# A searched instruction order, and remainder slots taken into the row-paired projections, in a fused attention and feed-forward kernel

## The chip, the cores and the metric

The kernel runs on one core of a Trainium2 chip. The metric is the time of the slowest core in microseconds (us), here that of the only one.

## The reference

An attention with random features (8 batches, 8 heads, 576 positions, 64 dimensions, 128 features) is followed by a gated feed-forward block on its 4608 output rows.

```python
def phi(x):                                   # x: q or k, scaled by D ** -0.25
    h = einsum('bhsd,md->bhsm', x, omega) - sum(x * x, -1, keepdims=True) / 2
    return exp(h - max(h, -1)) / sqrt(m)
q_p, k_p = phi(q_s), phi(k_s)
kv  = einsum('bhsm,bhsd->bhmd', k_p, v)
z   = sum(k_p, axis=2)
num = einsum('bhsm,bhmd->bhsd', q_p, kv)
den = einsum('bhsm,bhm->bhs', q_p, z)[..., None] + 1e-6
x   = (num / den).transpose(0, 2, 1, 3).reshape(4608, 512)

h   = x @ w_in                                # 512 -> 2048, the up-projection
g   = h * sigmoid(beta * h)
out = g @ w_out                               # 2048 -> 512, the down-projection
```

All inputs and the output are float32; the kernel computes its matmuls in bf16.

## The kernel before

The kernel is built in two steps. A first pass lists operations with their engine, an estimated duration and the tiles that they read and write. A greedy scheduler then simulates all engines, gives out the eight banks of PSUM (the memory that TensorE writes its results to) and fixes each engine's order. A table of small corrections to the priorities, found by a search, tunes that order.

```python
UPS = 2                                      # up and down blocks alternate in groups of this many
EARLY = 'q0 v0 q1 k1 w0 qm w2 w1 w3 o2 v1 o0 o1 o3'   # early loads: w = w_in, o = w_out, by chunk
HINTS = {1: 3, 3: -3, 8: -1, ...}            # (cut) priority corrections by number of the operation
...
        for op in self.ops:                  # in the scheduler
            op.prio += HINTS.get(op.seq, 0)
...
                places = {n: place(n) for n in (1, 2, 4)} if e == "PE" else None
```

`w_in` and `w_out` come in four chunks of 512 columns or rows each. They stand with the other early loads in the queue of GpSimd, in the order of `EARLY` as the scheduler then places them.

```python
    def load_w_out(c):
        dma("POOL", 0.8, 2.55,
            lambda e: e.dma_start(
                w_out_bf[:, 4 * c : 4 * c + 4, :],
                moe_w_out[c * 512 : (c + 1) * 512, :].rearrange("(f p) d -> p f d", p=128)),
            writes=[("wout", c)])
```

From batch 1 on, q and k are projected in two parts for each half of the positions. An "island" holds the main part: two matmuls of 64 rows each run beside each other, one on the upper and one on the lower half of the array's rows. Four banks take the results. The remainder slot (positions 512 to 575) is projected apart, as a matmul on the whole array with the block-diagonal `bd`, into a bank of its own.

```python
        def island(x, half):
            banks = [Use("att") for _ in range(4)]
            ...
                    for c in range(8):                       # k; q has 4 matmuls of 512 columns
                        for a in range(2):
                            rows = slice(64 * a, 64 * a + 64)
                            i = e.matmul(ps[:, banks[2 * a + c // 4].b, c % 4 * 128 : c % 4 * 128 + 128],
                                         src[rows, c // 4, c % 4, :], bd[rows, a, :], ...)
            ...                                              # then four exponentials on ScalarE
        def proj(x, half, i):                                # i = 4: the remainder
            ...                    # k: 1 matmul of 256 columns; q: 2 of 128; one exponential of 256
...
                    if b >= ISLAND:
                        island(x, half)
                        proj(x, half, 4)
```

The softmax here doesn't subtract the row's maximum and nothing guards it: scores larger than these inputs give would overflow.

## Time and profile before

| | |
|---|---|
| time before, median of the first 3 runs | 321.13 us (320.84 to 321.63) |
| span in the trace (first to last instruction) | 320.3 us |
| TensorE busy | 305.0 us, 95% |
| first down-projection starts | 41.73 us |
| from there to the end of the last matmul | 275.39 us |

A time is about 1.8 us longer than the span of the same execution. The traced execution was a slow one for this kernel: it took 322.06 us, 0.43 above the slowest of the three timed ones. The lines that show the bound stand in the prediction. The timeline of TensorE up to the first down-projection has as columns start in us, length in us, engine, line and operation, tiles and shapes, count, and in brackets the idle time ahead with what ended it:

```profile
31.01 1.90 PE L951 MATMUL ps<-xT,w_in_bf 128*128 128x512 bf16 x8 [0.86 <-DMA w_in_bf<-in_moe_w_in_dram]
...
38.89 2.76 PE L951 MATMUL ps<-xT,w_in_bf 128*128 128x512 bf16 x11
41.73 1.04 PE L983 MATMUL ps<-w_out_bf,g_sb 128*128 128x512 bf16 x4
```

The up-projections (L951) wait for chunk 1 of `w_in`, which is the third of the four in the queue, until 30.96 us. They then run through, and the first down-projection (L983) starts at 41.73. Everything up to there is called **the front** below; the rest is called **the body**. The same timeline, later, shows one k island and the two remainders behind it:

```profile
153.69 0.62 PE L641 MATMUL ps<-bd,kT 64*128 64x128 bf16 x16
154.24 0.39 PE L595 MATMUL ps<-bd,kT 128*128 128x256 bf16 x2
```

A recorded length holds the latency of the last matmul too, so block lengths are taken from start to start: 154.24 - 153.69 = 0.55 us for the island.

### The profile page before, as it was taken

The numbers are of one execution on the slowest core, as the hardware profiler recorded it, in microseconds if no ns is written. First come the engines' busy times: TensorE is split into PE (matmuls) and PEld (weight loads), VectorE is DVE, ScalarE is ACT, GpSimd is POOL, SyncE is SP. The second block draws the span as 40 slices with busy tenths as digits, with TensorE's granted clock in tenths as the row PEclk, the third lists the DMA queues.
The fourth block names the chain that finished last, engine by engine and source line by source line (L and its number), as shares of the span: only waits on it lengthen the run. The fifth ranks groups of instructions, "written<-read, shape, count | busy, mean of one in ns | idle before, by whom it ended". The sixth has DMA issues, their size and how long they took to land.

```text
span 320.3 us, 5797 instructions
## 1 busy us (share of the span) xinstructions
PE 305.0 (95%) x2283; PEld 155.2 (48%) x2322; DVE 175.3 (55%) x331; ACT 202.8 (63%) x352; POOL 98.8 (31%) x155
## 2 busy tenths in 40 slices
PE   4698999999999999999999999999999999999996
PEld 3574436544545544554445444544454444444444
DVE  1596776276756852587248824981488174344300
ACT  3686875599678647766687558665866284454411
POOL 8993061073338301930085008700330000000000
PEclk9999999999999999999999999999999999999999
DMA  6999999999649986998569776986320300000023
GB/s 94 182 194 206 200 201 145 231 166 139 119 128 130 161 148 147 124 165 150 147 105 173 125 135 128 174 119 148 100 74 8 70 33 36 33 33 33 35 73 90
DMA packets 89723, 39.25 MB, mean 123 GB/s; under 512 B 57296, under 2 KB 85216, under 8 KB 89696
## 3 DMA queue, kind: packets, MB, share of 16 engines
q0 software_dynamic: 40192, 18.36, 46.0%
q1 hardware_dynamic: 49424, 20.46, 28.1%
q8 instruction: 18, 0.29, 0.4%
q14 instruction: 9, 0.07, 0.1%
q10 hardware_dynamic: 80, 0.07, 0.1%
HBM read 36.77 MB, written 9.44 MB: 144 GB/s over the span
## 4 chain that ended last, share of the span: by engine, by line
PE 85%; DMA 8%; POOL 5%; issue 1%; ACT 0%; POOLq 0%
PE ps L983 39%; PE ps L951 35%; DMA w_out_bf<-in_moe_w_out_dram 8%; PE ps L812 3%; PE ps L649 2%; PE ps L772 2%; PE ps L641 2%; POOL w_in_bf L430 1%; POOL k_nat L413 1%; POOL q_nat L399 1%; POOL q_nat L388 1%; PE ps L595 1%; PE ps L767 1%; PE ps L605 0%; POOL v_nat L413 0%
## 5 line engine op out<-in xcount | busy, mean ns | idle before, releaser
L951 PE MATMUL ps<-xT,w_in_bf 128*128 128x512 bf16 x558 | 131.5, 379 | 2.5 <-DMA w_in_bf<-in_moe_w_in_dram 1.5
L983 PE MATMUL ps<-w_out_bf,g_sb 128*128 128x512 bf16 (+1 forms) x572 | 132.6, 373 | 1.4 <-issue 0.3
L964 ACT ACTIVATE th_sb<-ps,beta_sb 128x512 f32<-128x512 f32 x144 | 98.9, 688 | 48.0 <-PE ps L951 42.3
L968 DVE SCALAR_TENSOR_TENSOR g_sb<-th_sb,ps 128x512 bf16<-128x512 f32 x144 | 97.1, 683 | 53.8 <-ACT th_sb L964 52.6
L983 PEld LDWEIGHTS ps<-w_out_bf,g_sb 128*128 128x128 bf16 x592 | 55.3, 98 | 63.4 <-issue 3.8
L951 PEld LDWEIGHTS ps<-xT,w_in_bf 128*128 128x128 bf16 x576 | 54.0, 98 | 63.0 <-DMA w_in_bf<-in_moe_w_in_dram 1.9
L729 POOL TENSOR_TENSOR vsc<-v_nat,mk 128x512 bf16<-128x512 bf16 x28 | 29.0, 1051 | 116.1 <-DVE mk L686 116.1
L995 ACT ACTIVATE o_sb<-ps 128x512 f32<-128x512 f32 (+1 forms) x37 | 21.9, 591 | 40.6 <-PE ps L983 40.5
L673 DVE TENSOR_TENSOR mt<-E_sb 128x1152 bf16<-128x1152 bf16 (+2 forms) x20 | 12.4, 630 | 42.6 <-ACT E_sb L619 27.0
L660 ACT ACTIVATE qpT<-ps 128x512 bf16<-128x512 f32 x56 | 29.2, 602 | 7.3 <-PE ps L649 7.2
L660 ACT ACTIVATE E_sb<-ps 128x512 bf16<-128x512 f32 x56 | 29.7, 620 | 4.9 <-PE ps L641 4.9
L826 DVE TENSOR_TENSOR xn<-ps,rden 128x640 bf16<-128x640 f32 (+1 forms) x32 | 25.3, 798 | 0.2
L812 PEld LDWEIGHTS ps<-kvs,qpT 128*128 128x128 bf16 x312 | 12.4, 97 | 4.5
L812 PE MATMUL ps<-kvs,qpT 128*128 128x65 bf16 x312 | 13.2, 193 | 0.0
L797 DVE CAST kvs<-ps 128x260 bf16<-128x260 f32 x14 | 6.0, 428 | 11.6 <-PE ps L772 11.4
L684 DVE TENSOR_REDUCE mxE<-mt 128x18 f32<-128x576 bf16 x16 | 12.0, 750 | 0.4
L388 POOL DMA_DIRECT2D k_nat<-in_k_dram x7 | 6.9, 987 | 15.8 <-DMA qT<-q_nat 14.2
L399 POOL DMA_DIRECT2D q_nat<-in_q_dram x16 | 10.5, 676 | 3.8 <-PE ps L595 3.8
L622 ACT ACTIVATE qpT<-ps 128x256 bf16<-128x256 f32 (+1 forms) x20 | 10.1, 523 | 1.2 <-PE ps L812 1.2
L619 ACT ACTIVATE E_sb<-ps 128x256 bf16<-128x256 f32 (+1 forms) x20 | 9.6, 517 | 1.6 <-PE ps L595 1.6
L772 PE MATMUL ps<-vsc,E_sb 128*128 128x65 bf16 x224 | 10.2, 194 | 0.0
L772 PEld LDWEIGHTS ps<-vsc,E_sb 128*128 128x128 bf16 x224 | 9.2, 98 | 1.4
(67 smaller groups left out, 183.4 us busy)
## 6 DMA issues: line engine op xcount, KB each, us to landing
out_dram<-o_sb SPq DMA_DIRECT2D x32, 256.0 KB, 2.5
q_nat<-in_q_dram POOLq DMA_DIRECT2D x8, 512.0 KB, 8.9
k_nat<-in_k_dram POOLq DMA_DIRECT2D x7, 512.0 KB, 6.5
v_nat<-in_v_dram POOLq DMA_DIRECT2D x7, 512.0 KB, 8.9
w_in_bf<-in_moe_w_in_dram POOLq DMA_DIRECT2D x4, 512.0 KB, 17.0
w_out_bf<-in_moe_w_out_dram POOLq DMA_DIRECT2D x4, 512.0 KB, 25.2
out_dram<-o_sb SPq DMA_DIRECT2D x6, 128.0 KB, 2.3
k_nat<-in_k_dram POOLq DMA_DIRECT2D x4, 144.0 KB, 4.2
```

The costliest lines, as they stand in the source:

```text
L399: lambda e, hh=hh: e.dma_start(nat[x][hh * 64 : hh * 64 + 64, sn, 2048:].rearrange("p (h y) -> p h y", y=64), flat(x, b)[4 * hh : 4 * hh + ...
L660: lambda e, u=u, a=a, bk=bk: e.activation(dst[:, slot, 8 * u + a : 8 * u + 8 : 2, :], ps[:, bk.b, :].rearrange("p (c m) -> p c m", m=128), ...
L673: lambda e, lo=lo, hi=hi: e.tensor_tensor(mt1[:, lo:hi, :], E_sb[:, se, lo:hi, 0:64], E_sb[:, se, lo:hi, 64:128], ALU.max),
L729: lambda e, pr=pr: e.tensor_tensor(vsc[:, sv, pr, 0:8, 0:D].rearrange("p (h j) d -> p h j d", h=2), vh[:, :, half, pr, :].rearrange("p h ( ...
L772: i = e.matmul(to[:, 65 * hh : 65 * hh + 65], E_sb[:, se, 8 * hh + 4 * pr + j, :], vsc[:, sv, pr, 4 * hh + j, :], start=False, stop=j == 3 ...
L812: i = e.matmul(view[:, pr, 65 * j : 65 * j + 65], qpT[:, sq, 8 * hh + 4 * pr + j if j < 4 else 16 + pr, :], kvs[:, sk, pr, 65 * hh : 65 * ...
L826: lambda e: e.tensor_tensor(xn[:, sx, 5 * hh : 5 * hh + nj, :, :].rearrange("p j r d -> p r j d"), nv()[:, :, :, 0:64], rd.unsqueeze(3).to ...
L951: i = e.matmul(o, w_in_bf[:, 2 * hh + half, f * 128 : (f + 1) * 128], rhs, start=kc == 0, stop=kc == 3, skip_group_check=True)
L964: lambda e: e.activation(th_sb[:, ts, :], ps[:, hb.b, :], AF.Tanh, scale=beta_sb[:, f : f + 1]),
L968: lambda e: e.scalar_tensor_tensor(g_sb[:, gs, f, :], th_sb[:, ts, :], 1.0, ps[:, hb.b, :], ALU.add, ALU.mult),
L983: i = e.matmul(ps[:, ob.b, 0:nc_], g_sb[:, gs, f, sub * 128 : (sub + 1) * 128], w_out_bf[:, f, c0 : c0 + nc_], start=f == 0, stop=f == NFF ...
L995: lambda e: e.activation(o_sb[:, os_, 0:nc_], ps[:, ob.b, 0:nc_], AF.Copy, scale=0.5),
```

## The change

From batch 5 on the two remainder matmuls of a half leave the full array. One joins the island at its start on the upper row half, one at its end on the lower, each beside work of the other half. They share a fifth bank, so a semaphore keeps the second from starting before the first is done. The order was searched anew for this, with up and down blocks alternating in fours instead of eights, and `v1` stands ahead of chunk 2 of `w_out` in the list of early loads.

```diff
+WIDE = 5
-E_PRIO, M_PRIO, N_PRIO, O_PRIO = 1, 2, 1, 1
+E_PRIO, M_PRIO, N_PRIO, O_PRIO = 2, 2, 2, 1
-EARLY = 'q0 v0 q1 k1 w0 qm w2 w1 w3 o2 v1 o0 o1 o3'
-UPS = 2
-LATE, KLAG = 1.0, 0.4
+EARLY = 'q0 v0 q1 k1 w0 qm w2 w1 w3 v1 o2 o0 o1 o3'
+UPS = 1
+LATE, KLAG = 1.5, 0.4
 ...                                (the table HINTS is replaced as a whole; cut)
-                places = {n: place(n) for n in (1, 2, 4)} if e == "PE" else None
+                places = {n: place(n) for n in (1, 2, 4, 5)} if e == "PE" else None
 ...
+    s_rest, rests = es.enter_context(nc.semaphore(name="s_rest")), [0]
 ...
+        def wide_island(x, half):
+            banks = [Use("att") for _ in range(4)]
+            mixed = Use("att")
 ...                                (main: the same matmuls as in island; cut)
+            def rest(e, a):
+                rows = slice(64 * a, 64 * a + 64)
+                src, om = tr[x][rows, st, 16 + half, :], bd[rows, a, :]
+                return e.matmul(ps[:, mixed.b, 128 * a : 128 * a + 128],
+                                src if x == "k" else om, om if x == "k" else src,
+                                start=True, stop=True, skip_group_check=True)
+            def pm(e):
+                rest(e, 0).then_inc(s_rest, 1)
+                rests[0] += 1
+                for c in range(0, 8, 1 if x == "k" else 4):
+                    main(e, 1, c)
+                    main(e, 0, c)
+                e.wait_ge(s_rest, rests[0])
+                return rest(e, 1)
 ...                                (four exponentials of 512 columns and one of 256; cut)
-                    if b >= ISLAND:
+                    if b >= WIDE:
+                        wide_island(x, half)
+                    elif b >= ISLAND:
                         island(x, half)
                         proj(x, half, 4)
```

## The prediction

> **What bounds the kernel now.** I read the page from the top: engine shares, then the forty slices, then the waits of TensorE in two parts, then the chain of work that ended last, and last the groups and the ScalarE timeline of one batch. The page of the kernel before:
>
> ```profile
> PE 305.0 (95%) x2283; PEld 155.2 (48%) x2322; DVE 175.3 (55%) x331; ACT 202.8 (63%) x352; POOL 98.8 (31%) x155
> ...
> PE   4698999999999999999999999999999999999996
> ...
> PEclk9999999999999999999999999999999999999999
> ```
>
> TensorE is busy 95% of the span at an undisturbed clock. No other engine is over 63%. The low digits are all in the first five slices (each 8 us) and the last. Busy is not proof of useful work, so I asked what TensorE waits for before and after 41 us, when the first down-projection starts. Waits of TensorE, 0 to 41 us, then 41 us to the end:
>
> ```profile
> PE ps L550 <- DMA q_nat<-in_q_dram: 2.4, 1, 2.4
> PE ps L472 <- DMA o_sb<-in_omega_dram: 1.6, 1, 1.6
> PE ps L951 <- DMA w_in_bf<-in_moe_w_in_dram: 1.5, 2, 0.9
> ```
>
> ```profile
> PE ps L641 <- ACT E_sb L619: 0.4, 1, 0.4
> PE ps L983 <- issue: 0.3, 2, 0.2
> ```
>
> Early on it waits for inputs (another 2.7 us at the very start is for the identity matrix). From 41 us on it waits 0.7 us in 279. So there the end is set by how many matmul columns TensorE streams, and not by an order. A piece of the chain of waits in the time of batch 6, with start, duration and work, shows what stands there:
>
> ```profile
> 186.90 0.55 PE ps L641 x16
> 187.46 0.33 PE ps L595 x2
> 187.78 0.05 issue
> 187.83 1.67 PE ps L983 x7
> 189.51 0.22 PE ps L605 x4
> 189.73 1.73 PE ps L983 x8
> 191.46 0.54 PE ps L649 x4
> 192.00 1.83 PE ps L983 x8
> 193.83 0.55 PE ps L641 x16
> ```
>
> L641 and L649 are the row-paired projections of k and q (64 rows each, two at a time); L595 and L605 are the remainder slots, full-array matmuls. Eight 512-column matmuls take 1.73 us, 0.216 each. Where seven stand instead of eight a record is missing from the trace (572 of 592 for L983), so I don't call the 0.05 "issue" an idle. ScalarE, which empties the banks, is at the same time not tight:
>
> ```profile
> 187.50 2.06 ACT L660 ACTIVATE E_sb<-ps 128x512 bf16<-128x512 f32 x4 [1.69 <-PE ps L641]
> 189.54 0.60 ACT L995 ACTIVATE o_sb<-ps 128x512 f32<-128x512 f32 x1
> 190.04 0.38 ACT L619 ACTIVATE E_sb<-ps 128x256 bf16<-128x256 f32 x1
> ```
>
> Four exponentials take 2.06 us, and consecutive starts (190.04, then 190.30 for the next) put a 256-column one at 0.26 us.
>
> **What the Trainium skill says.** "TensorE: Matmul & The Clock Gate", section "Wait — 56ns, not 53.3ns?", gives a warm start-to-start of N/2.4 GHz plus some 2.5 ns. The trace agrees: between successive starts I find 0.216 us for 512 columns, 0.109 to 0.110 for 256, and 0.056 for 128. "TensorEngine Tiling (Array Packing)", section "Key Properties", says that a change of tiling mode drains the array. Agreed: from the last 512-column matmul to the first of a paired block is 0.312 instead of 0.216, and from the last of a k block to what follows 0.148 instead of 0.056, so some 0.19 us for entry and exit. The same page, "Gotcha 1: PSUM Pressure", says that different row tiles cannot use one bank at the same time and that software has to synchronize them. No trace before shows this, as before every row half has banks of its own; it is why the change puts a semaphore between the two remainder matmuls. The first page, "The mechanism" of row tiling, says matmuls start and end in program order, which I need for that wait to sit at the block's end only.
>
> **The change part by part.** For batches 5, 6 and 7:
> - Removed on TensorE, per batch: two k remainders of 256 columns (2 x 0.109) and four q remainders of 128 columns (4 x 0.056), 0.218 + 0.224 = 0.442 us. Three batches: 1.33 us, all of it on the path, as TensorE never waits there. No mode switch goes away, because the remainders ran in the full-array mode around them.
> - Added: each paired block gets one remainder at its start on one row half and one at its end on the other. Beside each runs work of the other half, so the block is one 128-column slot longer: 0.056 us. With k and q, two halves, three batches there are 12 blocks: 0.67 us. Net so far -0.66 us. Pairing only halves a small thing.
> - The wait between the two remainders. A 64-row matmul of 128 columns is recorded with 217 ns, and from the end of a matmul to the start of a waiting ScalarE instruction I find a median of 38 ns. So the first remainder is known to be done about 0.26 us into the block (an estimate from these two). The last is due at 8 x 0.056 = 0.45 us in k and 2 x 0.216 = 0.43 us in q; its weight load takes 0.094. That leaves some 0.08 us: hidden, narrowly. I put 0.1 us in all.
> - Evictions: four of 512 and one of 256 columns per block, before and after. ScalarE's work is the same. But five banks of eight are now taken at once instead of four and later one.
> - The order. The comparison of the two orders shows that up to the first down-projection nothing of weight moves: the four w_in loads are queued at the same place, the first w_out chunk that a down-projection needs (chunk 0) still comes after one other chunk and batch 1's v, and 56 up-projection matmuls stand ahead of the first down-projection in both. So the input waits stay. Afterwards up and down alternate in fours instead of eights, and in batches 5 to 7 sixteen down matmuls (3.45 us) stand between the k and the q block. There is at most 0.7 us of idle to win. The 0.4 us wait came of a k remainder straight before a k block in batch 3 at 86 us; in the new order these two stand apart. I take 0.3 us off.
> - The end is the same: 52 instead of 56 last full down matmuls with the 4 moved ahead, 32 half-width ones, an eviction, a store.
>
> Sum: 321.13 - 0.66 - 0.3 + 0.1 = 320.27, say **320.3 us**, 0.3% faster.
>
> **The rivals.**
> 1. *The new wait costs.* If TensorE's sequencer, once stopped at the semaphore, gives up the weight load ahead, each of 12 blocks pays perhaps 0.1 to 0.2 us: 1.2 to 2.4 us, so 321.4 to 322.6. For it: only some 0.08 us of slack by my estimate. Against it: the other 16 (or 4) matmuls are already queued, and leaving the mode drains anyway.
> 2. *Five banks at once make TensorE wait for ScalarE.* In half 1 of each of the three batches the q block follows the k block after only 8 down and up matmuls, one key-value product and 4 more: some 3.3 us. ScalarE has meanwhile four exponentials (about 2.0), one eviction (0.5), one of 256 columns (0.26) and one or two tanh (0.6 each, from consecutive starts): 3.4 to 4.0 us, beginning 0.3 us in. But three other banks exist and not all five must be the same. If it waits, 0.3 to 0.5 us three times, about 1 to 1.5 us: 321.3 to 321.8.
> 3. *The searched order wins more than I see*, by moving the early part: 1 to 2 us of the early waits, so 318.5. Against it: those waits end on transfers whose queue order is unchanged.
> 4. *A transfer becomes late*, as stores and transposes move. DMA is busy to 60 to 90% only until about 150 us, and from 41 us on TensorE waited for none. Unlikely.
>
> **Range and chances.** The three repeats before spread over 0.8 us (320.84 to 321.63). Rival 1 or 2 in part (one in three together) moves me to 321.5; rival 3 (one in ten) to 319 or less. So 319.2 to 321.5. Faster by over 2% means under 314.7 us; the removed work and all idle after 41 us together come to 1.4 us, so 2%. Slower by over 2% (over 327.6) needs every block to lose 0.5 us: 1%. Within 2%: 97%.
>
> **What the profile after would show.** TensorE's waits after 41 us still under 1 us, with none for ScalarE of over 0.2 us at the q blocks of batches 5 to 7 (rival 2 otherwise). In the chain a wide k block from its first to the next full matmul near 0.60 instead of 0.55 us, a wide q block near 0.60 instead of 0.54, and no idle before its last matmul (rival 1 otherwise). L595 and L605 with 6 and 12 matmuls fewer. The first down-projection still at 41.5 to 42 us and the same waits before it (rival 3 otherwise). The wait for a k remainder at 86 us gone. The prediction is wrong if the early part shifts by over 1 us, or if the blocks with the semaphore take over 0.7 us.

## More of the kernel before

VectorE takes a reciprocal of a maximum and multiplies four columns of it with a mask, while GpSimd scales v:

```python
            G.add("DVE", 0.14, lambda e: e.reciprocal(mk[:, se, :], mxE[:, se, :]), ...)
            G.add("DVE", 0.14,
                  lambda e: e.tensor_tensor(mko[:, se, :, :], own[...], mk[:, se, 16:18]..., ALU.mult), ...)
```

## The result, and the profile after

| | kernel before | changed kernel |
|---|---|---|
| time, median (range), runs | 321.27 us (320.84 to 321.63), 4 | 321.49 us (321.19 to 321.70), 4 |
| span in the trace | 320.3 us | 319.6 us |
| first down-projection starts (front) | 41.73 us | 41.60 us |
| from there to the end of the last matmul (body) | 275.39 us | 274.90 us |

The ratio of the two is 1.0006, with a 95% interval of 0.9989 to 1.0024. A ratio is the mean time of one kernel's fast runs over that of the other's of the same rounds, so it is not quite the ratio of the medians quoted. Nothing can be seen to have changed. The traced spans differ by 0.7 us all the same, and the runs by as much among themselves.

The page of the changed kernel, the engine totals and two of the forty-slice rows:

```profile
PE 308.4 (96%) x2324; PEld 156.2 (49%) x2324; DVE 176.1 (55%) x331; ACT 201.4 (63%) x352; POOL 98.7 (31%) x155
...
PE   3998989999999999999999999999999999999996
...
PEclk9999999999999999999999999999999999999999
```

The bound has not moved: TensorE is at 96%, no other engine above 63%, and the clock is undisturbed. The count of 2324 isn't comparable with 2283, because the trace before lacked some records. The four largest waits of TensorE, 0 to 41 us (line waited at, what it waited for, total us, times, longest):

```profile
PE ps L495 <- DVE identb L448: 2.7, 1, 2.7
PE ps L474 <- DMA o_sb<-in_omega_dram: 1.5, 1, 1.5
PE ps L1005 <- DMA w_in_bf<-in_moe_w_in_dram: 1.3, 2, 1.0
PE ps L553 <- DMA k_nat<-in_k_dram: 0.8, 1, 0.8
```

The same view of the changed kernel from 41 us to the end:

```profile
PE ps L1037 <- DMA w_out_bf<-in_moe_w_out_dram: 1.2, 1, 1.2
PE ps L1005 <- DVE g_sb L1022: 0.3, 1, 0.3
```

Two things in these answer to the waits before. The wait of 0.4 us at a k island (L641 before) is gone. In its place an up-projection waits 0.3 us for VectorE, and the first down-projection waits 1.2 us for `w_out`. The front of the changed kernel in its timeline:

```profile
29.80 1.90 PE L1005 MATMUL ps<-xT,w_in_bf 128*128 128x512 bf16 x8 [1.02 <-DMA w_in_bf<-in_moe_w_in_dram]
...
36.82 3.63 PE L1005 MATMUL ps<-xT,w_in_bf 128*128 128x512 bf16 x16
41.60 1.04 PE L1037 MATMUL ps<-w_out_bf,g_sb 128*128 128x512 bf16 x4 [1.16 <-DMA w_out_bf<-in_moe_w_out_dram]
```

Chunk 1 of `w_in` lands 1.2 us earlier here than in the trace before, and the up-projections end 1.2 us earlier. That is then lost again: TensorE stands for 1.16 us (1.32 from start to start) until chunk 0 of `w_out` is there. The wide k island, at the place where before has L641 and L595:

```profile
154.24 0.23 PE L689 MATMUL ps<-bd,kT 64*128 64x128 bf16 x1
154.24 0.67 PE L680 MATMUL ps<-bd,kT 64*128 64x128 bf16 x16
154.70 0.22 PE L689 MATMUL ps<-bd,kT 64*128 64x128 bf16 x1
154.85 3.63 PE L1037 MATMUL ps<-w_out_bf,g_sb 128*128 128x512 bf16 x16
```

The block takes 154.85 - 154.24 = 0.61 us instead of 0.55. The first remainder (L689) starts together with the first main matmul, and the last one 0.46 us into the block, with no idle time ahead of it.

### The profile page after: what moved, and what is told of

Read it like the earlier page. It is cut to its first block, busy times and chain, and to the rows that moved or that the text cites. A ratio compares the mean times of both kernels' runs of the same rounds, so it can differ in the third digit from the quotient of the medians.

```text
span 319.6 us, 5836 instructions
## 1 busy us (share of the span) xinstructions
PE 308.4 (96%) x2324; PEld 156.2 (49%) x2324; DVE 176.1 (55%) x331; ACT 201.4 (63%) x352; POOL 98.7 (31%) x155
## 4 chain that ended last, share of the span: by engine, by line
PE 85%; DMA 8%; POOL 5%; DVE 1%; issue 0%; ACT 0%; POOLq 0%
PE ps L1037 40%; PE ps L1005 35%; DMA w_out_bf<-in_moe_w_out_dram 8%; PE ps L864 3%; PE ps L824 2%; PE ps L652 1%; PE ps L644 1%; POOL w_in_bf L432 1%; PE ps L680 1%; PE ps L683 1%; POOL k_nat L415 1%; POOL q_nat L401 1%; PE ps L689 1%; POOL q_nat L390 1%; PE ps L819 0%; DVE mko L743 0%
## 5 line engine op out<-in xcount | busy, mean ns | idle before, releaser
L1005 PE MATMUL ps<-xT,w_in_bf 128*128 128x512 bf16 x576 | 135.3, 379 | 1.6 <-DMA w_in_bf<-in_moe_w_in_dram 1.3
L1037 PE MATMUL ps<-w_out_bf,g_sb 128*128 128x512 bf16 (+1 forms) x592 | 135.2, 374 | 1.2 <-DMA w_out_bf<-in_moe_w_out_dram 1.2
L1022 DVE SCALAR_TENSOR_TENSOR g_sb<-th_sb,ps 128x512 bf16<-128x512 f32 x144 | 96.7, 682 | 51.2 <-ACT th_sb L1018 49.9
L663 ACT ACTIVATE qpT<-ps 128x512 bf16<-128x512 f32 x32 | 17.8, 600 | 3.8 <-PE ps L652 3.8
L708 ACT ACTIVATE qpT<-ps 128x512 bf16<-128x512 f32 x24 | 13.2, 598 | 3.2 <-PE ps L689 3.2
L401 POOL DMA_DIRECT2D k_nat<-in_k_dram x14 | 9.4, 686 | 10.2 <-DMA qT<-q_nat 10.2
L875 DVE RECIPROCAL rden<-ps 128x10 f32<-128x10 f32 (+1 forms) x32 | 6.6, 211 | 7.2 <-PE ps L864 6.6
L390 POOL DMA_DIRECT2D k_nat<-in_k_dram x7 | 6.9, 982 | 11.3 <-DMA xT<-xn 11.3
```

Of the source, the lines that this page charges most:

```text
L401: lambda e, hh=hh: e.dma_start(nat[x][hh * 64 : hh * 64 + 64, sn, 2048:].rearrange("p (h y) -> p h y", y=64), flat(x, b)[4 * hh : 4 * hh + ...
L663: lambda e, u=u, a=a, bk=bk: e.activation(dst[:, slot, 8 * u + a : 8 * u + 8 : 2, :], ps[:, bk.b, :].rearrange("p (c m) -> p c m", m=128), ...
L708: lambda e, u=u, a=a, bk=bk: e.activation(dst[:, slot, 8 * u + a : 8 * u + 8 : 2, :], ps[:, bk.b, :].rearrange("p (c m) -> p c m", m=128), ...
L1005: i = e.matmul(o, w_in_bf[:, 2 * hh + half, f * 128 : (f + 1) * 128], rhs, start=kc == 0, stop=kc == 3, skip_group_check=True)
L1022: lambda e: e.scalar_tensor_tensor(g_sb[:, gs, f, :], th_sb[:, ts, :], 1.0, ps[:, hb.b, :], ALU.add, ALU.mult),
L1037: i = e.matmul(ps[:, ob.b, 0:nc_], g_sb[:, gs, f, sub * 128 : (sub + 1) * 128], w_out_bf[:, f, c0 : c0 + nc_], start=f == 0, stop=f == NFF ...
```

## The experiments

### Which part of a run is fixed: both kernels again

The first run repeats the changed kernel, with nothing altered, on another chip.

> The changed kernel, unaltered, to have a closer ratio and a second trace. Theory F (the early part caps it): TensorE runs out of up-projection work at about 40.3 us and waits for chunk 0 of w_out, which lands at 41 to 42 us as in the kernel before; from the first down-projection to the last matmul it takes 274.9 us (before 275.4). Ratio to before 0.998 to 1.002. Rival S (the semaphore or the five banks cost it): idle in or before the wide blocks of over 0.1 us each in this trace, and no wait at the first down-projection.

It took 321.22 us (320.24 to 321.93, 6 runs), ratio to before 1.0000 [0.9980, 1.0021]. Its traced execution, which took 320.24 us, has the first down-projection at 40.42 us and a body of 274.90 us. Before was run again as well, for another trace of it, and the changed kernel a third time:

> The kernel before, unaltered, for the noise and a second trace. Theory F (all of the spread from run to run is made before the first down-projection): from the first down-projection to the last matmul it takes 275.39 us within 0.05, and the first down-projection follows the landing of w_in chunk 1 by 10.5 to 10.8 us unless the queue loses time in between. Ratio to itself 1.000 with an interval of some 0.002 to either side.

> The changed kernel, unaltered, a third time, as ten runs of it average 321.25 us and the kernel before 321.1, though all traces have 0.5 us less for the changed kernel from the first down-projection on. Theory C (chance of the early queue): this batch averages 320.6 to 321.2, at or under the kernel before. Rival V (the changed early part is really later by some 0.5 us on average): again equal to or slower than the kernel before, 321.1 to 321.6.

Before took 320.93 us (320.82 to 321.39; ratio to itself 0.9995 [0.9982, 1.0009]) with the first down-projection at 41.13 us, of which 0.49 (0.65 from start to start) was a wait for `w_out`, and a body of 275.34. The changed kernel took 321.02 us (320.64 to 321.43; 0.9994 [0.9975, 1.0012]) with 40.81 and 274.89. So **the body is the same to 0.05 us** in every trace of a kernel (two of before, three of the changed one), and the spread between these executions lies in the front. A trace shows the body's gain of 0.45 to 0.5 us exactly where a few timed runs can't.

What is in the body can be accounted for. Each matmul gets its spacing by columns, N/2.4 GHz plus 2.5 ns, which the prediction takes from the Trainium skill and checks; each of 26 paired blocks gets 0.188 us for entering and leaving the mode (0.096 and 0.092 measured). What is left from the first down-projection to the start of the last matmul holds the waits. The body as quoted is 0.27 us longer, by the recorded length of that last matmul.

| body in us | columns | mode changes | left over (waits, rounding) |
|---|---|---|---|
| before (two traces) | 268.85 | 4.89 | 1.38, 1.33 |
| changed kernel | 268.19 | 4.89 | 1.54 |

The columns fell by the 0.66 us that the prediction worked out. The left-over didn't fall by 0.3 but grew by 0.16 to 0.21.

### One part of the change at a time

Wide islands in the old kernel: the code of `wide_island` is added, while constants, early loads and corrections stay as before. The numbering of the corrections is kept, so that up to batch 5 the order is the same.

```diff
+WIDE = 5
     def __init__(self):
+        self.nseq = 0            # numbers the operations as if the remainders were still apart
...
+                    if b >= WIDE:
+                        wide_island(x, half)
-                    if b >= ISLAND:
+                    elif b >= ISLAND:
```

> The kernel before with the wide blocks alone from batch 5 on; the order up to batch 5 is that of before, instruction for instruction on TensorE, and the order after it what the scheduler makes of it with the old hints. Theory F: the blocks are worth what was worked out, 0.66 us less TensorE work after the first down-projection, so 275.4 becomes 274.7 (0.998 in the ratio, 320.6 us against 321.3). Rival S: 0 to +1.5 us against before.

The searched order with narrow islands:

```diff
-WIDE = 5
+WIDE = 9                         # no batch has this number
...
-                  kp if x == "k" else qp,
+                  kp if x == "k" else qp, seq=G.nseq - 5 if b >= 5 else None,
```

> The changed kernel with its searched order, but narrow blocks and full-array remainders in all batches; TensorE's order up to batch 5 is that of the changed kernel. Theory F: 0.66 us more than the changed kernel from the first down-projection on (275.6), time about 322.1 us, ratio to before 1.001 to 1.004; the wait of about 1 us for chunk 0 of w_out is there as in the changed kernel. Rival S: the same or faster than the changed kernel.

Wide islands alone took 321.05 us (320.36 to 322.11; 1.0004 [0.9984, 1.0023]), the new order alone 321.18 us (320.82 to 323.23; 1.0014 [0.9988, 1.004]). Both have a body of 275.19 us. The expected bodies were 274.7 and 275.6, so both were missed. The times say nothing, the bodies do:

| left over in the body, us | old order | new order |
|---|---|---|
| narrow islands | 1.38, 1.33 | 1.18 |
| wide islands | 1.83 | 1.54 |

The new order takes 0.15 to 0.29 us of waits away with either kind of island. The wide islands add 0.36 to 0.50 us of waits with either set of corrections, and this eats over half of the 0.66 us that they save.

"Wide islands" means here: with the order that the scheduler then finds from batch 5 on. It isn't the order of the narrow ones. In the traces of the narrow kernels 8 down-projections stand between the k and the q island of the second half of a batch. With wide islands it is a key-value product and 12 up- and down-projections in the changed kernel, 16 in the old one. No run holds this order fixed while the islands change, so the cost of the five banks isn't separated from that of the new order around them.

Stops of over 0.1 us, taken from start to start, account for all the differences in this table: without them 0.73 to 0.77 us is left in each of the five traces. With narrow islands the old order stops for 0.43 us at the k island of batch 3 and for 0.20 or 0.15 us for chunk 1 of `w_out` at about 44 us; the new order stops once, for 0.46 us at 104.8 us. So with narrow islands the new order only trades one stop in the middle for another. What it wins is the wait for `w_out`, for which it asks later.

The waits of TensorE from 41 us on with wide islands in the old order name them:

```profile
PE ps L1040 <- issue: 1.0, 6, 0.2
PE ps L1008 <- DVE xn L881: 0.5, 2, 0.2
PE ps L646 <- ACT E_sb L624: 0.4, 1, 0.4
```

The same view of the new order with narrow islands:

```profile
PE ps L1008 <- DVE g_sb L1025: 0.5, 1, 0.5
```

L881 is VectorE's division of the numerators, which empties banks for the attention's result. From start to start I find three stops of 0.17 to 0.18 us behind it in the first (at 172, 205 and 238 us). The changed kernel has two: 0.165 at 172.0, behind the division, and 0.16 at 237.0, behind VectorE's gate product (L1022). With narrow islands there is none from batch 5 on. Two of 0.16 us make 0.33 of the 0.36 us, and the three make 0.53 where 0.45 to 0.50 was found. The waits view doesn't list them all: a matmul of 512 columns is recorded with 379 ns but the next starts after 216, so a stop of under some 0.16 us leaves no gap between records. It is seen only as 0.384 instead of 0.216 us between two starts. The "issue" lines are mostly places where a record is missing from the trace.

### ScalarE's fifth bank, or VectorE's

My first theory for these stops was the second rival of the prediction: the fifth bank waits for ScalarE, since its exponential stands behind other ScalarE work. So that exponential is put straight behind the four others:

```diff
+            late_rests.append((G.ops[-2], rest_op))
...
+    for fourth, then in late_rests:
+        order.remove(then)
+        order.insert(order.index(fourth) + 1, then)     # where other ScalarE work lay between
```

> The changed kernel; on ScalarE the eviction of the fifth bank of each wide block stands straight after the four other evictions instead of up to two tanh later, nothing else moves. Theory B (the 0.165 us wait of an up-projection at 172.0 us, batch 5, is for the fifth bank, whose eviction ended at 172.12): that wait is gone; the one at 237.0 us in batch 7 (which ended with a tanh and a VectorE product) may stay; first down-projection to last matmul falls from 274.90 to 274.6 to 274.75. Rival: ScalarE and VectorE are simply behind there, the tanh that now comes 0.26 us later moves the wait elsewhere, and 274.90 stays or grows.

The stop was still 0.165 us, the left-over 1.53 and the body 274.89. The fifth bank's exponential now ended at 172.22 us, VectorE's division ran from 172.58 to 173.40, and the matmul that waits started at 173.46 (the front of this run was 1.28 us longer, so this is the stop at 172 us). So it isn't ScalarE's fifth bank, and that theory fell. The likely reason is the other side of the shared eight banks: with five of them taken at once, a matmul more often has to take one that VectorE is still emptying. That is argued from the start times and not shown. No run shows the choice of banks by itself, and the other order of batches 5 to 7 is a rival that stands untested.

This single look (322.7 us against 321.25 for before beside it, state unknown) has something else in it. Its timeline of TensorE in the front:

```profile
28.58 0.28 PE L921 MATMUL ps<-kvs,qpT 128*128 128x130 bf16 x2
30.99 1.51 PE L1007 MATMUL ps<-xT,w_in_bf 128*128 128x512 bf16 x5 [2.13 <-DMA w_in_bf<-in_moe_w_in_dram]
```

And the busy times of 30 to 35 us in it (window, length, then PE, PEld, DVE, ACT and POOL busy with counts, granted clock, DMA share, GB/s), followed by those of the changed kernel's first trace:

```profile
30.00:35.00 5.00, 4.01 (x27) 1.96 (x28) 1.27 (x2) 1.59 (x3) 0.00 (x0) 0.69 1.45 197
```

```profile
30.00:35.00 5.00, 5.00 (x40) 2.38 (x39) 3.33 (x7) 3.78 (x7) 0.00 (x0) 1.00 1.45 197
```

Chunk 1 of `w_in` was late, and TensorE idled for 2.13 us, of which 0.99 lie in this window. The mean granted clock of the window fell to 0.69, with 27 matmuls instead of 40. From the landing of the chunk to the end of the up-projections it took 11.93 us, against 10.52 in ten other traces, so 1.4 us were lost on top of the wait. One run of the narrow experiment (323.23 us) has the same mean clock of 0.995; it has no trace. "TensorE: Matmul & The Clock Gate", section "What's actually happening", says that the clock is throttled after an idle window of some 3.4 us which runs freely; here 2.13 us of idle was enough. Two stretches of some 3.41 us of this trace:

```profile
28.44:31.85 3.41, 1.28 (x8) 0.53 (x7) 1.91 (x5) 1.31 (x3) 0.55 (x1) 1.00 1.30 205
31.86:35.26 3.40, 3.40 (x24) 1.57 (x23) 0.84 (x2) 1.85 (x3) 0.00 (x0) 0.50 1.48 193
```

The whole idle time fell into the first stretch, and the clock was halved for the second and full again after it. Not every long idle does this: the trace of before has one of 2.38 us at 11.48 and stays at full clock. If windows of 3.41 us are counted on from the start of full clock in that trace (8.64 us), a border at 12.05 cuts it into 0.57 and 1.81. (In the throttled trace the first full clock, 11.37 to 31.85 us, is six such windows long.) The trace of the wide islands alone has 1.81 us idle in one window too, and full clock. So in these traces the border lies between 1.81 and 2.13 us of idle in one window; the clock was halved inside the work in one of them only.

### The small product beside GpSimd

The other stop in the changed kernel is 0.45 us at 104.6 us (the waits view gives 0.3 for it, by the end of the recorded matmul ahead). Its timeline there, all engines, cut to five lines:

```profile
102.31 2.09 POOL L781 TENSOR_TENSOR vsc<-v_nat,mk 128x512 bf16<-128x512 bf16 x2
102.50 0.43 DVE L849 CAST kvs<-ps 128x260 bf16<-128x260 f32 x1 [0.77 <-PE ps L824]
102.85 1.58 DVE L743 TENSOR_TENSOR mko<-own,mk 128x4 f32<-128x4 f32 x1
104.35 1.27 DVE L1022 SCALAR_TENSOR_TENSOR g_sb<-th_sb,ps 128x512 bf16<-128x512 f32 x2
105.08 1.25 PE L1005 MATMUL ps<-xT,w_in_bf 128*128 128x512 bf16 x5 [0.28 <-DVE g_sb L1022]
```

A VectorE product of four columns takes 1.58 us. From batch 2 on it takes 0.10 to 0.19 us elsewhere, and in batch 1 it takes 1.00 and 0.69. The one here starts inside GpSimd's first product and ends just after GpSimd's second product (104.40). The gate product behind it is late, and the up-projection waits for its bank. "SBUF — State Buffer", section "🔬 SBUF: two separate sides", describes this: VectorE and GpSimd share a pair of ports, which one of them holds for a whole instruction while the other stands still. It names VectorE operations with two inputs in SBUF among those concerned, as this product is. The trace agrees: the two slow ones of batch 1 as well end within 0.02 us of the end of a GpSimd product. It also shows more: this one, started during GpSimd's first product, wasn't done before the second had ended too. In the next kernel the small product comes straight behind the reciprocal that it needs, ahead of GpSimd's work:

```diff
+            pairs.append((mk_op, mko_op))
...
+    for first_, then in pairs:
+        order.remove(then)
+        order.insert(order.index(first_) + 1, then)
```

> The changed kernel; on VectorE the 4-column product mko of each half-batch stands straight after the reciprocal that it needs, nothing else moves. In the changed kernel's trace that product took 1.58 us at 102.85 us instead of some 0.1 to 0.2, beside two GpSimd products of 1 us, and the up-projection behind it waited 0.45 us at 104.6. Theory P (the two engines' common access holds the small product up, and that wait is the searched order's own): that instruction takes under 0.3 us there, the 0.45 us wait is gone, and first down-projection to last matmul falls from 274.90 to 274.4 to 274.5 us. Rival: it is slow for another reason (it waits for its input), and the 274.90 stays within 0.05.

In this single look (319.61 us, state unknown, before beside it 321.25) all these products take 0.16 us and the stop at 104.6 is gone. VectorE around 169 us, however, and after it TensorE:

```profile
169.39 0.16 DVE L744 TENSOR_TENSOR mko<-own,mk 128x4 f32<-128x4 f32 x1
169.47 0.82 DVE L880 TENSOR_TENSOR xn<-ps,rden 128x640 bf16<-128x640 f32 x1
```

```profile
170.34 0.82 PE L1007 MATMUL ps<-xT,w_in_bf 128*128 128x512 bf16 x3 [0.20 <-DVE xn L880]
```

Here the product now stands directly ahead of the division, and TensorE's stop behind the division grew from 0.165 to 0.364 us, by about the length of the product. The body is 274.64 us: 0.26 shorter, not 0.45. That is a second piece of evidence that this stop ends on VectorE. The time of this look is mostly its front (40.01 us).

### The front: in which order the weights come

In all traces the early loads come one after the other, about 2.5 us for each chunk of 512 KB. At one place per trace, which differs from run to run, 0 to 1.1 us more goes by. The up-projections end 10.52 us after chunk 1 of `w_in` lands (10.52 to 10.53 in ten traces), and chunk 0 of `w_out`, with three other loads between the two, lands some 10.75 us after it or later. So with either order the first down-projection can only wait for `w_out`: in nine of ten traces it starts 0.05 us after that chunk lands (the tenth is the look with the throttled clock). The page of before shows this in its section 4, where `DMA w_out_bf<-in_moe_w_out_dram` holds 8% of the chain of work that ended last. To test that, chunks 0 and 1 of `w_out` are queued ahead of `v1` and chunks 2 and 3 in the changed kernel. Nothing on the other engines is moved.

```diff
+    loads = {n: G.ops[i : i + (3 if n == "v1" else 1)] for n, i in placed.items()}
+    names = 'o0 o1 v1 o2 o3'.split()
+    at_ = sorted(order.index(op) for n in names for op in loads[n])
+    for i, op in zip(at_, [op for n in names for op in sorted(loads[n], key=order.index)]):
+        order[i] = op
```

> The changed kernel with one thing moved: in the queue of early loads the chunks 0 and 1 of w_out go ahead of batch 1's v and chunk 2 (0, 1, v, 2, 3 in place of v, 2, 0, 1, 3). The order on TensorE is untouched. Theory F: chunk 0 lands about 6 us sooner (some 35 us), the 1.2 us wait at the first down-projection is gone, the first down-projection starts at about 40.3 us and the time falls by 0.8 to 1.2 us against the changed kernel: 320.3 to 320.7 us, ratio to before 0.997. Rival J (where the queue's time is lost is chance and TensorE has to wait elsewhere): no gain, the wait turns up later at chunk 1, at batch 1's v or at the next loads.

It took 320.57 us (320.10 to 320.77; 0.9981 [0.9965, 0.9996]), with no wait at the first down-projection (40.37 us) and the body unchanged (274.89), as expected. The wait for chunk 1 of `w_in` is still there. So the next three kernels queue all of it in the order of use, in both kernels, with `names = 'w1 w2 w3 o0 o1 v1 o2 o3'`. The third of them also has the small product behind its reciprocal, in batches 0 to 4 only.

> The kernel before, with the early loads queued in the order of their use: w_in chunks 0, 1, 2, 3, w_out 0, 1, batch 1's v, w_out 2, 3 (before: w_in 0, 2, 1, 3, w_out 2, v, w_out 0, 1, 3); the order on TensorE is untouched. Theory F: w_in chunk 1 lands 2.5 us sooner, the wait of some 0.9 us for it goes, the first down-projection is no longer tied to w_out: 0.9 to 1.5 us less, 319.6 to 320.2 us, ratio 0.995 to 0.997, with less spread. From the first down-projection on 275.4 as before. Rival J: the gain is lost at a later early load, ratio 0.998 to 1.001.

> The changed kernel with the same queue order (w_in 0, 1, 2, 3, w_out 0, 1, v, w_out 2, 3). Theory F: both kernels now have an equal early part, so what the change is worth after the first down-projection can be read from the times: 0.5 us less than the kernel before with that queue (ratio between the two 0.9985), 319.1 to 319.7 us; from the first down-projection on 274.9. Rival: as for the kernel before with that queue.

> The changed kernel with that queue order and with mko straight after its reciprocal in batches 0 to 4 only, so that the wait at 104.6 us goes and batch 5 is left as it was. Expected: from the first down-projection to the last matmul 274.45, time 0.45 us less than the changed kernel with that queue, 318.7 to 319.3 us, ratio to before 0.992 to 0.995: the fastest of all. Rival: the wait only moves, 274.9, and the time is that of the changed kernel with that queue.

| | time, us (range) | ratio to before [95%] | front | body |
|---|---|---|---|---|
| before, loads in order of use | 320.48 (319.97 to 320.98) | 0.9978 [0.9963, 0.9993] | 39.67 | 275.79 |
| changed, loads in order of use | 319.05 (318.71 to 319.39) | 0.9933 [0.9920, 0.9947] | 39.22 | 274.89 |
| the same, small product moved | 318.51 (317.47 to 319.20) | 0.9915 [0.9895, 0.9934] | 39.27 | 274.43 |

The front of the changed kernel with the loads in order of use:

```profile
28.63 0.28 PE L921 MATMUL ps<-kvs,qpT 128*128 128x130 bf16 x2
28.75 1.89 PE L1007 MATMUL ps<-xT,w_in_bf 128*128 128x512 bf16 x8
...
35.75 3.63 PE L1007 MATMUL ps<-xT,w_in_bf 128*128 128x512 bf16 x16
39.22 1.03 PE L1039 MATMUL ps<-w_out_bf,g_sb 128*128 128x512 bf16 x4
```

No gap is left from 28.63 us to the first down-projection. With the old order it isn't as good:

```profile
41.17 1.90 PE L985 MATMUL ps<-w_out_bf,g_sb 128*128 128x512 bf16 x8
43.51 1.04 PE L985 MATMUL ps<-w_out_bf,g_sb 128*128 128x512 bf16 x4 [0.44 <-DMA w_out_bf<-in_moe_w_out_dram]
```

The old order runs twelve down-projections in this stretch and asks for chunk 2 of `w_out` before it is there (43.47 us). The searched order, which alternates in fours, asks later. Here the change is worth 320.48 - 319.05 = 1.4 us, of which the body gives 0.9 (0.44 of that is this wait) and the front 0.45. Of the front's share 0.29 us is that chunk 0 of `w_in` landed earlier in that one trace (24.35 instead of 24.64), for no reason that the runs show. Both expectations were missed: the wait for chunk 2 kept before above its 319.6 to 320.2 us, and the two kernels differ by 1.4 us instead of 0.5. The best kernel took 318.51 us, 2.7 us below the mean of before.

Is the front of the changed kernel worse than that of before? In the changed kernel `v1` stands ahead of chunk 2 of `w_out`; the last kernel puts it behind again, as before has it (`names = 'o2 v1 o0 o1 o3'`).

> The changed kernel with the early queue of the kernel before (w_out chunk 2 ahead of batch 1's v, all else as changed; chunk 0 of w_out is still behind both). Theory C: the same time as the changed kernel beside it, within 0.2%. Rival V by way of the queue (putting v first delays chunk 0): some 0.5 us faster than the changed kernel beside it.

It took 320.70 us (320.03 to 321.84; 0.9986 [0.9965, 1.0007]), mean 320.87, against a mean of 321.17 for the changed kernel. The standard errors are 0.27 and 0.12, so this decides nothing.

## Why the prediction was right or wrong

The verdict held, and the range by luck: 321.49 us at first, 0.01 below its upper end. Over all runs the mean is 321.17 us for the changed kernel (16 runs) and 321.17 for before (43 runs). The gain of 0.86 us in the prediction's sum isn't there. Step by step:

- **The bound** was read rightly: columns and mode changes make 273.7 of the 275.1 us up to the last matmul. The reading that TensorE waits for no transfer from 41 us on was not right: before waits 0.24 us for `w_out` at 41.73 and 0.20 at 44.31, which the view hides. The 0.3 us of "issue" that it did count are missing records.
- **Removed and added columns**, -0.66 us: right. The block lengths were foretold as 0.60, and measured as 0.61 and 0.59 to 0.60. L595, now L598, has 26 matmuls of 256 columns instead of 32, and L605, now L608, 20 of 128 columns instead of 32.
- **The wait between the two remainders**, "I put 0.1 us in all": it was nothing. The last remainder starts 0.46 us into the block without a gap. Rival 1 is refuted by the same reading.
- **The order**, "I take 0.3 us off": 0.15 to 0.29 us, but for another reason. The wait at 86 us is gone, as foretold, and its place is taken by the 0.45 us behind the small VectorE product, so that this trade wins nothing. With narrow islands the gain is the wait for chunk 1 of `w_out` that the prediction didn't see.
- **Five banks at once** is the term of the sum that was mis-sized: zero in the sum, and only a rival (of 1 to 1.5 us) with ScalarE as the cause. The wide islands, with the order that comes with them, measured 0.36 to 0.50 us. The second rival was right that a wait comes with them and wrong about whom it is for: ScalarE was tested at one of the stops and cleared, and all five stops found end on VectorE, four of them on its division. Whether it is the five banks or the order around them that costs this isn't shown. The prediction said "That leaves some 0.08 us: hidden, narrowly" of the semaphore and looked there; the wait came elsewhere.
- **The front**, "So the input waits stay": the places stay, the lengths don't. "The first down-projection still at 41.5 to 42 us" took one trace as fixed; the traces of the two kernels show 40.42 to 41.73, and with the two looks that have only small edits 40.0 to 42.9. By the prediction's own sign ("if the early part shifts by over 1 us") one trace of the changed kernel, 1.3 us earlier, would have refuted it; but three traces of one kernel differ by 1.2 us among themselves, so the sign couldn't tell. The other sign, waits of under 1 us after 41 us, failed in the first trace with 1.5 us, of which 1.2 was the first down-projection's wait for `w_out`. This is where the rest of the gain would have to be: the body gives 0.47 us and the mean times give none. An estimate from the means (time less 1.8 us, less the body, less 3.1 us after the last matmul) puts the front of before at 40.87 and that of the changed kernel at 41.34 us on average, 0.47 us later with a standard error of 0.14. The few traces rather show the opposite (chunk 0 of `w_out` lands at 40.37 to 41.55 us in the changed kernel, at 41.09 and 41.68 in before), and the last run didn't settle it. A throttled clock as in the single look isn't the cause: all 16 runs have a mean clock of 0.999 or more. So **whether and why the front got longer stays open**, and with it over half of the missing gain (0.47 of 0.86 us).
- **Rival 3**, that the searched order wins in the front, did not come true. The 319.05 us near its 318.5 came of another edit, the queue in the order of use.

## What to carry to other kernels

When a trace has a fixed part and a part that varies from run to run, find the border first: here the body can be compared to 0.05 us from one trace each, while the times of 4 to 6 runs hide a gain of 0.5 us. Take waits from start to start, since a view by recorded lengths can hide stops of 0.2 us. A block that takes more banks at once should be charged for what the other users of the banks may lose, whichever engine empties them, and for the order that the scheduler has to change around it. Here the waits at the start ended on a queue, and sorting that queue by first use was worth more (2.1 us in the changed kernel, 0.7 in before) than all the instructions saved in the change.

## What the Trainium skill lacked or had wrong

- "TensorE: Matmul & The Clock Gate", section "What's actually happening", ties the throttling to an idle window of some 3.4 us. Here 2.13 us of idle in a stretch of 3.41 us halved the granted clock over the next 3.41 us and cost 1.4 us more, so the window needn't be idle as a whole; 1.81 us in one window did nothing, in two traces. No run shows more of the rule.
- "SBUF — State Buffer" has the lock between VectorE and GpSimd right, but says in its summary that the second to issue is blocked until the first finishes. Here a product of four columns, begun beside one GpSimd product, was by the recorded spans held over the next one as well: 1.58 us instead of the usual 0.10 to 0.19.
- "TensorEngine Tiling (Array Packing)" says that a change of mode drains the array, without a size: 0.096 us on the way in and 0.092 on the way out. It also asks for synchronization of two row tiles that use one bank: a semaphore between two matmuls with 0.46 us of other work between them cost nothing.
- No page that I read gives the time in which chunks in one queue of GpSimd follow each other: about 2.5 us for 512 KB each, with up to 1.1 us more at one place per trace. The fronts in the traces move with it.
